# Step 0's first two pairs of an attention and feed-forward kernel: 64-key diagonal blocks and a carried state in place of full 128-key scores

## The chip, the cores and the metric

One core of one Trainium2 chip. The metric is the time of one execution on the device in microseconds; for the kernel before it is the median of 3 runs. The kernel is one program: every engine gets a fixed list of instructions, and semaphores make one engine wait for another.

## The reference

The first stage is a gated linear attention, B = 4, H = 8 heads, S = 768 positions, head size D = 48; the second a feed-forward layer on its output, 3072 tokens, 384 to 2048 to 384.

```
f = sigmoid(f_logit)
for t in range(S):
    state = f[t] * state + k[t] (outer) v[t]      # per batch and head, 48 x 48
    y[t] = q[t] @ state
x = y as (B * S, H * D)
h = x @ w_in
g = h where h >= 1, 0 where h <= -1, (h + 1)**2 / 4 between
out = g @ w_out
```

All inputs and the output are float32; the weights reach the chip as 64-bit words.

## The kernel before

**Steps, pairs, units.** Time is cut in 6 steps of 128 positions (C = 128, half of it T = 64). Heads go in 4 pairs per step, so pair n is pair n % 4 of step n // 4. A step's output is the x of the second stage, which is 16 units per step, one for every 128 columns of the hidden layer, so 96 units, numbered through. A unit is nine f16 products of 128x512 into `ph` (line 370, or 1041 for unit 0) and, two units later, nine into `po` (line 389). Attention of step i + 1 is put between the units of step i.

**How a pair is computed.** Gates make running products by scans on VectorE (lines 601 and 608), and keys and queries are multiplied by them (611, 613). For steps 1 to 5 two pairs go together: `both` (774) are the scores of 64 keys with 64 queries, in four diagonal blocks per batch; `parts` (978) sums keys times values over each half of the step; `begin` and `part` (863) are the masked scores times values of the second and of the first half; `before` (895) is the queries times the state that came before them. Between halves the state is handed on as `later`.

**Step 0 before the change.** It has no state before it, and its pairs 0 and 1 use full scores of 128 keys by 128 queries: `scores` (695), a mask on VectorE for each pair and head (739), and `first` (heads, 1007), the masked scores times values. Their keys are turned by TensorE (`turn`, 800) and kept, and `states(0)` makes the state for step 1 from them in one piece of 32 products (957), between units 4 and 5, with `states(2)`, for pairs 2 and 3, behind it. Pair 3 is spread over the rows of three gates: `last` (726) adds its scores up. `second` (1007 and 1019) is the values' part of pairs 2 and 3. The third gate (m = 2) is done in two halves of the batch, and so are the scores that need it.

**What sets the order.** A planner (class Plan) gives every operation a cost from the table COST, works out from the end how late each may be, and lets each engine take the ready one with the least slack. On TensorE every operation depends on the one that was added before it, so its order is the order in which the list START, then the units, then the places between units, name their work. TURNS says beside which unit a pair's keys are turned, VISITS at which units two pairs' scores and sums, their begin and their end stand (a half is behind that unit's second products), AFTER what else follows a unit. Where the planner expects TensorE to idle it puts in products of zeros (459). INSTRUCTIONS counts loads and products of a kind, since code comes in blocks.

```
START = (("scores", 0), ("mask", 0, 0), ("mask", 0, 1), ("last", 0), ("turn", 0), ("scores", 1), ("mask", 1, 0), ...
         ("scores", 2, 0), ("last", 2, 0), ("scores", 2, 1), ("last", 2, 1), ("first", 0),
         ("mask", 2, 1), ("mask", 3, 1), ("first", 1), ("second", 0), ("second", 2), ("mask", 2, 0), ("mask", 3, 0), ("second", 3))
INSTRUCTIONS = dict(scores=32, scores_half=16, heads=32, thirds=32, thirds_of_two=64, both=128, begin=64, ... parts=128, ... turn=8)
AFTER = {4.5: (('states', 0), ('states', 2)), 2: (('turn', 2), ('turn', 3))}
```

**Weights and their tests.** A weight piece comes by DMA (issued by SP, line 411), ScalarE takes its top byte (`bits`, 497), VectorE joins the rest (499), ScalarE rounds the high half (503), VectorE subtracts for the low half (504). Units need both. Besides, the fast path holds only if the inputs lie within bounds: `small_piece` loads each of the 16 weight blocks again, and four reductions each (523) find their least and greatest; `norms_of` squares on ScalarE, turns (822) and sums (823) on VectorE; the result is a flag that is read at the end. These are put wherever an engine is free.

Of the kernel before, what the change touches and what calls it, by code (L numbers as in the profile page):

```python
# [24 lines left out]
C = 128  # L25
NI = S // C
NP = H // 2
R = 112
# [31 lines left out]
W = 2 * DM  # L60


SMALL_PRODUCTS = ("scores", "scores_half", "heads", "thirds", "thirds_of_two", "both", "begin", "before", "before_half", "part", "states", "parts", "parts_last")
# [3 lines left out]
COST = dict(mm=216, narrow=114, scores=1000, scores_half=500, heads=940, thirds=940, thirds_of_two=940, half=330, both=940, begin=430, before=880, part=450, states=700, before_half=440, parts=730, parts_last=730, zeros=4860, turn=395, first=160, last=200,  # L67
            rows=316, turned_rows=150, scan=1140, dve=602, small=200, sums=467, gate=600, act=575, bits=660, round=485, copy=520, turned=412, sig=538, decay=226,
            issue=480, near=600, least=300)

# [10 lines left out]
def JOINED(n):  # L81
    return 65 + 1.055 * n


INSTRUCTIONS = dict(scores=32, scores_half=16, heads=32, thirds=32, thirds_of_two=64, both=128, begin=64, before=128, before_half=64, part=64, states=64, parts=128, parts_last=64, zeros=24, turn=8)
BLOCK, FIRST_BLOCK, AHEAD, BEHIND, FETCH, OFFSET, WAITS = 256, 193, 48, 40, 4800, 9, 1.0045


# [6 lines left out]
VISITS = {4: (7.0, 7.0, 11.0, 11.0), 6: (11.0, 12.5, 12.5, 12.5), 8: (22.0, 22.0, 24.5, 24.5), 10: (24.5, 27.5, 27.5, 27.5), 12: (33.0, 33.0, 37.0, 37.0), 14: (37.0, 43.5, 43.5, 43.5), 16: (48.0, 48.0, 51.0, 51.0), 18: (51.0, 55.5, 55.5, 55.5), 20: (68.0, 68.0, 75.0, 75.0), 22: (75.0, 75.0, 76.0, 76.0)}  # L95
# [29 lines left out]
class Plan:  # L125
# [7 lines left out]
    def add(self, engine, cost, emit, *deps, kb=0, count=None, many=0):  # L133
        flat, made = [], count is not None

        def spread(d):
            if isinstance(d, list):
                for e in d:
                    spread(e)
            elif d is not None and d not in flat:  # L140
                flat.append(d)

        spread(list(deps))
        cost, kind = COST[cost] if isinstance(cost, str) else cost, cost
# [12 lines left out]
        if engine == "PE":  # L157
            self.tensor = o
        self.ops.append(o)
        return o  # L160
# [96 lines left out]
def gla_moe(ctx: ExitStack, tc: tile.TileContext, ff, kqd, f0, vv, vad, vbd, wd, fixedd, gates, values, headsd, out):  # L257
# [75 lines left out]
    def wide(a):  # L333
        return a.rearrange("r b c -> r (b c)")
# [93 lines left out]
    def fresh(t):  # L428
        nc.gpsimd.memset(t, 0.0)
# [133 lines left out]
    def old(n, *names, of=att):  # L563

        return [] if n < 0 else [of[n].get(k) for k in names]
# [141 lines left out]
    am_of = [am[0:2], am[2:4], [am[0], act_f[0][:, 0:N].rearrange("r (b c) -> r b c", b=B)], [am[2], opening[2]]]  # L707
    last_held = [bank(6), bank(4)]

    def scores_of_last(t, some=ALL):  # L710
# [21 lines left out]
    def masks(n, h):  # L732

        c = att[n]
        c.setdefault("am", [None, None])
        b, ps, _ = c["held"][h]
        t = am_of[n][h]
        free = {(2, 0): lambda: att[0]["ys"][0], (3, 0): lambda: att[0]["ys"][0], }.get((n, h), lambda: None)
        o = vec("dve", lambda: nc.vector.tensor_tensor(
            out=t, in0=ps, in1=mask.rearrange("u (o t) -> u o t", o=1).broadcast_to([C, B, C]), op=ALU.mult),  # L740
            c["sc"], ready["mask"], free())
        banks[b][:] = [o]
        c["am"][h] = o

# [6 lines left out]
        return [by_block(t) for t in am[n // 2 % 2 * 2:][:2]]  # L751

    TILES = ((0, 0), (1, 1), (1, 0), (0, 1))

    def borrowed(k):

# [208 lines left out]
    def states_by_parts(n, k, alone):  # L965

        i, p = pairs[n]
        c, d = att[n], att[n + 1]
        held = [bank(0), bank(1)] if alone else borrowed(k)
        sums = [wide(b[1])[:R, 0:2 * B * D] for b in held]  # L970

        def emit():
            for e in range(2):
                for m, (q, t) in enumerate(blocks(n + e)):
                    a = (e * B + m) * D
                    for l, h in (TILES if i < NI - 1 else TILES[1:3]):
# [5 lines left out]
        o = vec("sums", lambda: nc.vector.tensor_tensor(out=later[:, 0:2 * B * D], in0=sums[0], in1=ds[n // 2 % 2][:, 0:2 * B * D], op=ALU.add),  # L982
                c["st"], c["db"], d["db"], old(n - 2, "y", "se"))
# [168 lines left out]
    for n in range(NP):  # L1152
        prepare(n)

    def of_first(t):
        att[0].setdefault("ys", []).append(heads(t, lambda m, e: va[:, m, 2 * e + t], [am_of[e][t] for e in range(2)], [att[e]["am"][t] for e in range(2)], [att[0]["lv"], banks[firsts[t][0]]]))
        att[0]["y"] = att[1]["y"] = att[0]["ys"][-1]
# [15 lines left out]
    work = dict(mask=masks, scores=lambda n, *h: scores(n, ((0, 1), (3, 2), (5, 7))[n], *[HALF[k] for k in h]), last=lambda t, *h: scores_of_last(t, *[HALF[k] for k in h]), first=of_first, second=of_second,  # L1173
                turn=lambda n: transpose_tensor(n, (5, 5, None, None)[n]), states=lambda n: states(n), rows=lambda n: transpose_rows(n))
    for kind, *n in START:
        work[kind](*n)
# [55 lines left out]
    for u in range(NI * NJ):  # L1232
        unit_1(u)
        attend(u)
        if u >= BEHIND_BY:
            unit_2(u - BEHIND_BY)
        attend(u + 0.5)
    for c in range(NJ):
        small_piece(c)
    for j in range(NJ):  # L1240
        norms_of(j)
    tested, again = test()
    fits = nc.alloc_registers("fits")
    registers = {r.engine: r for r in fits.handles}
# [166 lines left out]
```

## Time and profile before

| | |
|---|---|
| time, median of 3 runs | 444.78 us (444.38 to 445.21) |
| the profiled execution's own time | 444.19 us |
| its span, first to last instruction | 442.5 us |
| TensorE busy | 436.3 us, 99%, 4537 products and 4537 loads of weights |
| VectorE busy | 333.2 us, 75% |
| ScalarE busy | 223.8 us, 51% |
| GpSimd busy | 35.3 us, 8% |
| DMA | 53.30 MB, mean 120 GB/s |

The profile is of one execution. Products are pipelined: in a list in order of time, the step from one start to the next is what a product costs, and its printed length holds a run-out that the next one hides. A share of busy time says little of TensorE here; whether it waits is seen in the starts. Line numbers are those of the kernel before.

### The profile page before, as it was taken

The page shows a single profiled execution, that of the slowest core. Times are in us where ns is not written, and L with a number is a line of the kernel's source. Part 1 is how long each engine was busy: PE and PEld are TensorE (multiplying, and loading weights), DVE is VectorE, ACT ScalarE, POOL GpSimd, SP SyncE. Part 2 cuts the span into 40 slices and gives each one's busy share as a digit, 9 for nine tenths or more (in the row PEclk, how much of TensorE's full clock was granted, in tenths as well). Part 3 has the DMA queues.
Part 4 walks back from the last instruction along what each step waited for, and adds up shares of the span by engine and source line. Part 5 has one row for each costly group of instructions (what it writes and reads, how often), then busy time and mean ns, then how long its engine had stood idle before and what let it go on. Part 6 is the DMA issues. An engine that isn't in the chain of part 4 may idle for free.

```text
span 442.5 us, 10884 instructions
## 1 busy us (share of the span) xinstructions
PE 436.3 (99%) x4537; PEld 222.2 (50%) x4537; DVE 333.2 (75%) x664; ACT 223.8 (51%) x428; POOL 35.3 (8%) x77
## 2 busy tenths in 40 slices
PE   8999999999999999999999999999999999999996
PEld 4845545544554545544545545444444654444442
DVE  7979999899989898899999898499667836111111
ACT  4589899645535545355535274345434433533332
POOL 5103120102001011011001011000000000000000
PEclk9999999999999999999999999999999999999999
DMA  7879988542304413086322342171100000100002
GB/s 275 304 286 419 362 302 287 187 120 82 99 8 150 115 37 108 1 291 219 101 54 77 122 140 77 51 228 70 71 2 1 3 21 0 73 0 0 1 0 75
DMA packets 18003, 53.30 MB, mean 120 GB/s; under 512 B 3072, under 2 KB 3712, under 8 KB 17952
## 3 DMA queue, kind: packets, MB, share of 16 engines
q1 hardware_dynamic: 17952, 52.59, 34.9%
q8 instruction: 36, 0.59, 0.5%
q14 instruction: 15, 0.12, 0.1%
HBM read 44.70 MB, written 4.72 MB: 112 GB/s over the span
## 4 chain that ended last, share of the span: by engine, by line
PE 95%; DVE 0%; ACT 0%; issue 0%
PE po L389 42%; PE ph L370 42%; PE pa L863 2%; PE pa L895 2%; PE ph L774 2%; PE pa L978 1%; PE pa L800 1%; PE pa L774 0%; PE ph L1041 0%; PE pa L1007 0%; PE pa L957 0%; PE ph L978 0%; PE pa L1019 0%; PE po L1019 0%; DVE w_lo_usual L399 0%; ACT w_lo_usual L393 0%
## 5 line engine op out<-in xcount | busy, mean ns | idle before, releaser
L389 PE MATMUL po<-g_usual,w_hi_usual 128*128 128x512 f16 x866 | 201.9, 379 | 0.0
L382 ACT ACTIVATE act<-ph,lifted 128x512 f32<-128x512 f32 x96 | 65.8, 686 | 172.3 <-PE ph L370 169.6
L389 PEld LDWEIGHTS <-w_hi_usual 128*128 128x128 f16 x866 | 83.9, 98 | 100.0
L370 PEld LDWEIGHTS <-w_hi_usual 128*128 128x128 f16 x855 | 83.2, 98 | 99.4
L370 PE MATMUL ph<-x_usual,w_hi_usual 128*128 128x512 f16 x567 | 132.5, 379 | 0.0
L1058 DVE TENSOR_TENSOR g_usual<-act,g_usual 128x512 f16<-128x512 f32 x96 | 66.1, 689 | 79.2 <-ACT g_usual L1057 77.7
L814 DVE STREAM_TRANSPOSE kn<-kq 32x128 f32<-32x128 f32 x224 | 67.8, 302 | 3.3
L370 PE MATMUL ph<-w_lo_usual,w_hi_usual 128*128 128x512 f16 x288 | 67.4, 379 | 0.0
L1057 ACT CAST g_usual<-act 128x512 f16<-128x512 f32 x96 | 59.2, 617 | 2.4
L605 POOL COPY end<-w 128x4 f32<-128x4 f32 (+1 forms) x20 | 8.5, 426 | 227.3 <-DVE w L601 227.2
L601 DVE TENSOR_TENSOR_SCAN w<-f,least_w 128x512 f32<-128x512 f32 (+1 forms) x18 | 20.8, 1157 | 1.8 <-ACT f L597 1.8
L608 DVE TENSOR_TENSOR_SCAN f<-f,rec 128x512 f32<-128x512 f32 (+1 forms) x18 | 20.7, 1157 | 0.2
L523 DVE TENSOR_REDUCE ok<-raw 128x1 f32<-128x384 f32 x40 | 19.6, 536 | 0.0
L504 DVE SCALAR_TENSOR_TENSOR w_hi_usual<-bits,w_hi_usual 128x768 f16<-128x768 f32 (+1 forms) x20 | 15.6, 790 | 1.4 <-ACT w_hi_usual L503 1.4
L503 ACT ACTIVATE w_hi_usual<-bits 128x768 f16<-128x768 f32 (+1 forms) x20 | 14.0, 714 | 1.6 <-DVE bits L499 1.5
L618 POOL TENSOR_TENSOR kq<-end,f0s 128x4 f32<-128x4 f32 x18 | 13.4, 745 | 4.0 <-ACT f0s L581 2.5
L863 PE MATMUL pa<-am,v 64*64 64x64 f32 x624 | 13.6, 221 | 0.0
L863 PEld LDWEIGHTS pa<-am,v 64*64 64x64 f32 x624 | 11.3, 134 | 4.2 <-issue 3.8
L597 ACT ACTIVATE f<-f 128x513 f32<-128x513 f32 (+2 forms) x18 | 10.8, 603 | 4.7 <-DMA f<-in_f 4.7
L822 DVE STREAM_TRANSPOSE w_lo_usual<-w_lo_usual 128x384 f32<-128x384 f32 x22 | 12.6, 573 | 0.5
L393 ACT ACTIVATE w_lo_usual<-po 128x512 f32<-128x512 f32 (+1 forms) x18 | 10.5, 584 | 4.2 <-PE po L389 3.2
L611 DVE TENSOR_TENSOR kq<-kq,w 128x512 f32<-128x512 f32 (+1 forms) x20 | 12.4, 619 | 0.0
(137 smaller groups left out, 368.6 us busy)
## 6 DMA issues: line engine op xcount, KB each, us to landing
kq<-in_kq SPq DMA_DIRECT2D x18, 512.0 KB, 4.6
raw<-in_w SPq DMA_DIRECT2D x8, 767.6 KB, 7.0
raw<-in_w SPq DMA_DIRECT2D x7, 768.0 KB, 5.9
raw_late<-in_w SPq DMA_DIRECT2D x6, 768.0 KB, 4.3
out_y<-w_lo_usual SPq DMA_DIRECT2D x17, 256.0 KB, 2.1
f<-in_f SPq DMA_DIRECT2D x16, 256.5 KB, 3.2
v<-in_v SPq DMA_DIRECT2D x10, 384.0 KB, 4.5
raw_late<-in_w SPq DMA_DIRECT2D x4, 767.6 KB, 9.3
```

The lines of the kernel that those rows point to most:

```text
L370: nc.tensor.matmul(ps[:, to], w_in((ws or (w_hi, w_lo))[1 - high], j, kt), xt[t][:, kt, c], start=(n == 0), stop=(n == 8))
L382: nc.scalar.activation(a, ps, AF.Square, bias=lifted, scale=0.5 * 2.0 ** (UP_G // 2 - UP))
L389: nc.tensor.matmul(po[e][:, c], w_out((ws or (w_hi, w_lo))[part], j, e), g[:, c], start=(j == 0 and n == 0 and c.start == 0), stop=(j == N ...
L503: h = sca(ROUNDED(n), lambda: nc.scalar.activation(hi, val, AF.Copy, scale=2.0 ** UP_W), v)
L504: l = vec(JOINED(n), lambda: nc.vector.scalar_tensor_tensor(out=lo, in0=val, scalar=2.0 ** UP_W, in1=hi, op0=ALU.mult, op1=ALU.subtract), h)
L523: seen.append(vec(JOINED(DM), lambda at=at, op=op, b=b, e=e: nc.vector.tensor_reduce(out=ok[:, at:at + 1], in_=words_of(mem)[1][:, b:e].bi ...
L601: s1 = vec(COST["scan"] if count == 1 else 602, lambda bwd=bwd, u0=u0, u1=u1: nc.vector.tensor_tensor_scan(out=wide(w[:, u0:u1]), data0=bw ...
L608: s2 = vec(COST["scan"] if count == 1 else 602, lambda fwd=fwd, b0=b0, b1=b1: nc.vector.tensor_tensor_scan(out=fwd, data0=fwd, data1=wide( ...
L814: nc.vector.transpose(kn_of(n)[u:u + 32, ::-1, r:r + 32], src[:, :, u:u + 32])
L863: nc.tensor.matmul(held[h][1][64 * e:64 * e + 64, m, T * (1 - k):][:, :T], v_of[pr // 2][half, a:a + 64], masked(n)[h][half, block], start ...
L1057: o = g["hi"] = sca("copy", lambda: nc.scalar.copy(hi, a), o, unit_out.get(k - HOMES_G))
L1058: g["lo"] = vec("dve", lambda: nc.vector.tensor_tensor(out=lo, in0=a, in1=hi, op=ALU.subtract), o, unit_out.get(k - HOMES_G))
```

## The change

Pairs 0 and 1 of step 0 take the form of the later steps. Their scores are made in 64-key diagonal blocks for both pairs into the same two banks (`both_of_first`), with two masks for both pairs. `parts_of_first` sums keys times values over the two halves right in the opening; ScalarE copies the first half's sums twice (once padded, as the state that the second half's queries read) and the second half's once, and VectorE adds the two for step 1's state, so `states(0)` goes. `of_first` has three pieces: `begin`, `before` and `part`. The first warm-up is 10 products and two that clear the two banks. Loads and squares of the weights' tests wait until unit 64's first products are done. TURNS and VISITS get new numbers, for nearly all pairs.

```diff
-TURNS = {4: 6.5, 6: 10.5, 8: 21.0, 10: 26.5, 12: 32.5, 14: 41.5, 16: 46.0, 18: 51.5, 20: 60.5, 22: 72.5}
-VISITS = {4: (7.0, 7.0, 11.0, 11.0), 6: (11.0, 12.5, 12.5, 12.5), 8: (22.0, 22.0, 24.5, 24.5), 10: (24.5, 27.5, 27.5, 27.5), ...
-START = (("scores", 0), ("mask", 0, 0), ("mask", 0, 1), ("last", 0), ("turn", 0), ("scores", 1), ("mask", 1, 0), ("mask", 1, 1), ("turn", 1), ("last", 1),
-         ("scores", 2, 0), ("last", 2, 0), ("scores", 2, 1), ("last", 2, 1), ("first", 0),
-         ("mask", 2, 1), ("mask", 3, 1), ("first", 1), ("second", 0), ("second", 2), ("mask", 2, 0), ("mask", 3, 0), ("second", 3))
+TURNS = {4: 7.0, 6: 10.5, 8: 21.0, 10: 25.0, 12: 31.5, 14: 41.0, 16: 45.5, 18: 53.0, 20: 63.5, 22: 72.0}
+VISITS = {4: (8.0, 8.0, 11.0, 11.0), 6: (11.0, 12.5, 12.5, 12.5), 8: (22.0, 22.0, 23.5, 23.5), 10: (23.5, 26.5, 26.5, 26.5), ...
+START = (("last", 0), ("both", 0), ("turn", 0), ("turn", 1), ("both", 1), ("parts",), ("last", 1),
+         ("scores", 2, 0), ("last", 2, 0), ("first", "begin"), ("scores", 2, 1), ("last", 2, 1), ("first", "before"), ("first", "part"),
+         ("mask", 2, 1), ("mask", 3, 1), ("second", 0), ("mask", 2, 0), ("second", 2), ("mask", 3, 0), ("second", 3))
-AFTER = {4.5: (('states', 0), ('states', 2)), 2: (('turn', 2), ('turn', 3))}
+CHECKED = 4, 0
+WARM = 10
+AFTER = {4.5: (('states', 2),), 2: (('turn', 2), ('turn', 3))}
...
-    add("PE", "zeros", lambda: warm(12), set_zeros)
+    def cleared():
+        warm(WARM)
+        for t in (po[0], wide(pa[2])):
+            nc.tensor.matmul(t, zeros, zeros..., start=True, stop=True)
...
+    set_ds.append(add("POOL", 600, lambda: fresh(first_half)))
...
+    first_two = [bank(0), bank(1)]
+    def both_of_first(e):
+        def emit():
+            for m, (q, b) in enumerate(blocks(e)):
+                for k, h in TILES:
+                    (a, z), half = HEADS[h], slice(T * k, T * k + T)
+                    nc.tensor.matmul(by_block(first_two[h][1])[half, e * B + m], key(e, q, b)[a:z, half],
+                                     query(e, q, b)[a:z, T * (1 - k):][:, :T], start=True, stop=True)
+        c = att[e]
+        c["sc"] = add("PE", "both_half", emit, c["kq"])
+        if e == 0:
+            return
+        for h, (b, ps, _) in enumerate(first_two):
+            o = vec("dve", ... masked(0)[h] = by_block(ps) * mask_t ..., c["sc"], ready["mask_t"])
...
+    def parts_of_first():
+        held = [bank(3), bank(2)]
+        sums = [wide(b[1])[:R, 0:2 * B * D] for b in held]
...
+        c["st"] = d["st"] = add("PE", "parts", emit, c["kn"], d["kn"], c["lv"])
+        c["later"] = [sca(412, ... first_half[r:z, ...] = sums[0][r:z] ...) for (r, z), y in zip(HEADS, (0, PAD))]
+        c["sum"] = sca(412, lambda: nc.scalar.copy(later[:, 0:2 * B * D], sums[0]), c["st"])
+        c["rest"] = sca(412, lambda: nc.scalar.copy(second_half, sums[1]), c["st"])
+        banks[3], banks[2] = [c["later"], c["sum"]], [c["rest"]]
+    def of_first(what):
...
+        if what == "begin":
+            o = add("PE", "begin", lambda: attended_of(True), c["am"], c["lv"], banks[3], banks[2])
+            c["yb"] = sca("small", lambda: nc.scalar.copy(seen_y..., held[0][0:1, :, T - 2:T]), o)
+        elif what == "before":
+            c["ys"] = d["ys"] = add("PE", "before_half", before, c["yb"], c["later"], set_ds)
+        else:
+            c["y"] = d["y"] = add("PE", "part", lambda: attended_of(False), c["yb"])
+            o = vec("sums", ... state = second_half + later ..., c["y"], c["sum"], c["rest"])
...
+    first_of = len(plan.ops)
     for c in range(NJ):
         small_piece(c)
     for j in range(NJ):
         norms_of(j)
+    behind = unit_in[CHECKED]
+    for o in plan.ops[first_of:]:
+        if o.engine == "SP" or o.engine == "ACT":
+            o.deps.append(behind)
```

## Rows read from the trace of the kernel before

**Rows 1.** Busy time by stage: stretch, length, each engine's busy us, clock, DMA, GB/s
```profile
10.00:20.00 10.00, 9.17 (x138) 7.23 (x138) 10.00 (x22) 5.21 (x9) 2.57 (x6) 1.00 0.94 371
...
21.90:37.90 16.00, 16.00 (x79) 7.70 (x80) 13.47 (x23) 14.76 (x28) 0.99 (x1) 1.00 0.85 323
...
80.00:300.00 220.00, 220.00 (x2469) 110.57 (x2462) 196.17 (x426) 105.73 (x219) 18.96 (x36) 1.00 0.36 112
...
372.00:438.20 66.20, 66.20 (x309) 30.05 (x307) 12.29 (x19) 23.68 (x37) 0.00 (x0) 1.00 0.03 12
```

**Rows 2.** TensorE in order of time, 38 to 70 us: start, length, line, operation
```profile
38.23 0.93 PE L957 MATMUL pa<-sd,kn 128*48 128x48 f32 x32
38.99 0.89 PE L957 MATMUL pa<-v,am 128*48 128x48 f32 x32
...
47.59 0.93 PE L800 MATMUL pa<-ident,kq 112*128 112x112 f32 x8
48.36 2.11 PE L370 MATMUL ph<-x_usual,w_hi_usual 128*128 128x512 f16 x9
...
51.38 0.90 PE L978 MATMUL pa<-v,kn 64*48 64x48 f32 x64
52.21 2.12 PE L389 MATMUL po<-g_usual,w_hi_usual 128*128 128x512 f16 x9
...
68.63 0.69 PE L863 MATMUL pa<-am,v 64*64 64x64 f32 x32
69.14 0.22 PE L774 MATMUL ph<-kq 48*64 48x64 f32 x1
```

**Rows 3.** TensorE in order of time, 15 to 22 us, the opening's end
```profile
15.33 0.37 PE L695 MATMUL po<-kq 48*128 48x128 f32 x1
...
15.88 0.27 PE L726 MATMUL ph<-kq,w_lo_usual 64*128 64x128 f32 x1
...
16.53 1.09 PE L1007 MATMUL po<-am,sd 128*64 128x128 f32 x16
...
18.75 0.30 PE L1019 MATMUL po<-act,v 128*32 128x128 f32 x1
...
21.82 2.12 PE L1041 MATMUL ph<-x_usual,w_hi_usual 128*128 128x512 f16 x9
```

**Rows 4.** VectorE in order of time, 15 to 19 us: the first and the sixth mask
```profile
15.20 0.68 DVE L739 TENSOR_TENSOR am<-pa,fixed 128x512 f32<-128x512 f32 x1
...
18.19 0.68 DVE L739 TENSOR_TENSOR w_lo_usual<-po,fixed 128x512 f32<-128x512 f32 x1
```

**Rows 5.** Line 895 from 69.5 to 73 us: least, median, greatest ns, first and last start
```profile
L895 PE MATMUL pa<-kq,later x32: 218/218/218, 70.1 to 70.5; 48*64 48x64 f32 x32
```

**Rows 6.** ScalarE in order of time near 40 us: the copy behind states(0)
```profile
40.28 0.47 ACT L961 COPY sd<-pa 112x384 f32<-112x384 f32 x1
```

**Rows 7.** TensorE in order of time: first products of units 64 and 80
```profile
302.03 2.11 PE L370 MATMUL ph<-x_usual,w_hi_usual 128*128 128x512 f16 x9
...
372.04 2.10 PE L370 MATMUL ph<-x_usual,w_hi_usual 128*128 128x512 f16 x9
```

**Rows 8.** The tests: line 523 behind 300 us by stage; groups of 822 and 823
```profile
300.00:443.00 143.00, 9.63 (x20) 1.00 0.06 22
...
L822 DVE STREAM_TRANSPOSE w_lo_usual<-w_lo_usual 128x384 f32<-128x384 f32 x22 | 12.6, 573 | 0.5
...
L823 DVE TENSOR_REDUCE w_lo_usual<-w_lo_usual 128x4 f32<-128x384 f32 x22 | 12.0, 547 | 0.4
```

**Rows 9.** ScalarE and VectorE in order of time, 43 to 49 us: unit 7's weights
```profile
43.39 1.00 ACT L497 ACTIVATE bits<-raw_late,top_of 128x768 uint32<-128x768 fp8e4 x1
...
46.19 0.93 DVE L499 SCALAR_TENSOR_TENSOR bits<-raw_late,bits 128x768 uint32<-128x768 uint32 x1
...
47.34 0.86 ACT L503 ACTIVATE w_hi_usual<-bits 128x768 f16<-128x768 f32 x1
```

**Rows 10.** The page's DMA queues: packets, MB, share; TensorE's code
```profile
q8 instruction: 36, 0.59, 0.5%
```

More of the change, by code (lines that the diff above doesn't have):

```diff
@@ L60 @@
 W = 2 * DM
-SMALL_PRODUCTS = ("scores", "scores_half", "heads", "thirds", "thirds_of_two", "both", "begin", "before", "before_half", "part", "states", "parts", "parts_last")
+SMALL_PRODUCTS = ("scores", "scores_half", "heads", "thirds", "thirds_of_two", "both", "both_half", "begin", "before", "before_half", "part", "states", "parts", "parts_last")
 HOP, LANDING, PER_KB, LANES, FIRST, RISE = 200, 1350, 2.75, 8, 500, 700
 LATENCY = dict(PE=235, ACT=140, DVE=110, POOL=150)
-COST = dict(mm=216, narrow=114, scores=1000, scores_half=500, heads=940, thirds=940, thirds_of_two=940, half=330, both=940, begin=430, before=880, part=450, states=700, before_half=440, parts=730, parts_last=730, zeros=4860, turn=395, first=160, last=200,
+COST = dict(mm=216, narrow=114, scores=1000, scores_half=500, heads=940, thirds=940, thirds_of_two=940, half=330, both=940, both_half=470, begin=430, before=880, part=450, states=700, before_half=440, parts=730, parts_last=730, zeros=4860, turn=395, first=160, last=200,
             rows=316, turned_rows=150, scan=1140, dve=602, small=200, sums=467, gate=600, act=575, bits=660, round=485, copy=520, turned=412, sig=538, decay=226,
@@ L82, in JOINED @@
     return 65 + 1.055 * n
-INSTRUCTIONS = dict(scores=32, scores_half=16, heads=32, thirds=32, thirds_of_two=64, both=128, begin=64, before=128, before_half=64, part=64, states=64, parts=128, parts_last=64, zeros=24, turn=8)
+INSTRUCTIONS = dict(scores=32, scores_half=16, heads=32, thirds=32, thirds_of_two=64, both=128, both_half=64, begin=64, before=128, before_half=64, part=64, states=64, parts=128, parts_last=64, zeros=24, turn=8)
 BLOCK, FIRST_BLOCK, AHEAD, BEHIND, FETCH, OFFSET, WAITS = 256, 193, 48, 40, 4800, 9, 1.0045
@@ L737, in masks @@
         t = am_of[n][h]
-        free = {(2, 0): lambda: att[0]["ys"][0], (3, 0): lambda: att[0]["ys"][0], }.get((n, h), lambda: None)
         o = vec("dve", lambda: nc.vector.tensor_tensor(
             out=t, in0=ps, in1=mask.rearrange("u (o t) -> u o t", o=1).broadcast_to([C, B, C]), op=ALU.mult),
-            c["sc"], ready["mask"], free())
+            c["sc"], ready["mask"])
         banks[b][:] = [o]
@@ new lines, in parts_of_first, with emit @@
+    def parts_of_first():
+        c, d = att[0], att[1]
+        held = [bank(3), bank(2)]
+        sums = [wide(b[1])[:R, 0:2 * B * D] for b in held]
+        def emit():
+            for e in range(2):
+                for m in range(B):
+                    a = (e * B + m) * D
+                    for l, h in TILES:
+                        (r, z), half = HEADS[h], slice(T * l, T * l + T)
+                        nc.tensor.matmul(sums[1 - l][r:z, a:a + D], kn_of(e)[half, m, r:z], values_of(e, h)(m)[half], start=True, stop=True)
+        c["st"] = d["st"] = add("PE", "parts", emit, c["kn"], d["kn"], c["lv"])
+        c["later"] = [sca(412, lambda r=r, z=z, y=y: nc.scalar.copy(first_half[r:z, :, y:y + D], sums[0][r:z].rearrange("r (g c) -> r g c", c=D)), c["st"], set_ds)
+                      for (r, z), y in zip(HEADS, (0, PAD))]
+        c["sum"] = sca(412, lambda: nc.scalar.copy(later[:, 0:2 * B * D], sums[0]), c["st"])
+        c["rest"] = sca(412, lambda: nc.scalar.copy(second_half, sums[1]), c["st"])
+        banks[3], banks[2] = [c["later"], c["sum"]], [c["rest"]]
@@ new lines, in of_first, with attended_of, before @@
+    def of_first(what):
+        c, d = att[0], att[1]
+        held = [f[1] for f in firsts[:2]]
+        def attended_of(other):
+            for m in range(B):
+                for e, k in TILES:
+                    h, half = 1 - k if other else k, slice(T * k, T * k + T)
+                    nc.tensor.matmul(held[h][64 * e:64 * e + 64, m, T * (1 - k):][:, :T], va[half, m, 2 * e + h], masked(0)[h][half, e * B + m],
+                                     start=other and m == 0, stop=m == B - 1, skip_group_check=not other)
+        def before():
+            for m in range(B):
+                for e, h in TILES:
+                    (r, z), (q, b) = HEADS[h], blocks(e)[m]
+                    nc.tensor.matmul(held[h][64 * e:64 * e + 64, m, T:], first_half[r:z, e * B + m], query(e, q, b)[r:z, T:], start=False, stop=False, skip_group_check=True)
+        if what == "begin":
+            o = add("PE", "begin", lambda: attended_of(True), c["am"], c["lv"], banks[3], banks[2])
+            c["yb"] = sca("small", lambda: nc.scalar.copy(seen_y.rearrange("u (b c) -> u b c", b=B), held[0][0:1, :, T - 2:T]), o)
+            c["yb"].early = PROMPT
+        elif what == "before":
+            c["ys"] = d["ys"] = add("PE", "before_half", before, c["yb"], c["later"], set_ds)
+        else:
+            c["y"] = d["y"] = add("PE", "part", lambda: attended_of(False), c["yb"])
+            s = state[:, 0:2 * B].rearrange("r b e -> r (b e)")
+            o = vec("sums", lambda: nc.vector.tensor_tensor(out=s, in0=second_half, in1=later[:, 0:2 * B * D], op=ALU.add), c["y"], c["sum"], c["rest"])
+            c["se"] = d["se"] = state_of[0, 0] = [o]
@@ L1171, in of_second @@
             x_of[0, t] = rounded(firsts[t][0], wide(firsts[t][1]), lambda t=t: [x_at(0)[n][:, t] for n in range(2)], y, None)
-    work = dict(mask=masks, scores=lambda n, *h: scores(n, ((0, 1), (3, 2), (5, 7))[n], *[HALF[k] for k in h]), last=lambda t, *h: scores_of_last(t, *[HALF[k] for k in h]), first=of_first, second=of_second,
+    work = dict(mask=masks, both=both_of_first, parts=parts_of_first, scores=lambda n, *h: scores(n, ((0, 1), (3, 2), (5, 7))[n], *[HALF[k] for k in h]), last=lambda t, *h: scores_of_last(t, *[HALF[k] for k in h]), first=of_first, second=of_second,
                 turn=lambda n: transpose_tensor(n, (5, 5, None, None)[n]), states=lambda n: states(n), rows=lambda n: transpose_rows(n))
```

20 lines of the change are left out of this document (14 added, 6 removed).

## The prediction

> **What bounds the kernel now.** First the table of stages: behind 21.9 us TensorE is busy for every microsecond of a stretch (16.00 of 16, 220.00 of 220, 66.20 of 66.2), at the full granted clock, 2.4 GHz [rows 1]. The reader then goes to the order of products, because a busy share hides stalls: the nine products of the unit at 48.36 take 2.11 us with the last one's run-out, and no gap stands between a unit and the small products beside it [rows 2]. So behind the first product of unit 0, at 21.82 [rows 3], the time is a plain sum of what TensorE issues, plus an end (438.2 to the last instruction) that the change leaves alone. Two things alone can move the time: what is taken out of that sum or held up within it, and the moment at which unit 0 begins.
>
> What sets that moment is read from VectorE: it is busy for 10.00 of the 10 us from 10 to 20 [rows 1]. At 15.20, right behind the third gate's last product, it begins to mask scores; the masks are 0.60 apart, (18.19 - 15.20) / 5 [rows 4]. TensorE waits for them: `first` for head 0 starts at 16.53, just behind the second mask, and `second` at 18.75, just behind the sixth; then it runs through to unit 0 in 21.82 - 18.75 = 3.07 us [rows 3]. There are eight masks in all.
>
> **The change, part by part.**
>
> *The states of pairs 0 and 1 leave the stream.* `states(0)` ran between units 4 and 5, from 38.23 to 38.99; `states(2)` follows it directly and stays [rows 2]. With the stream gapless, 0.76 us go. The switch into and out of small products is paid by `states(2)` as before. The new places move small products between units, but their number and kind stay: each pair of pairs still has its visit, its begin and its end, and the turns of pairs 4 to 7 stay on TensorE. I cost that at nothing as long as their inputs come in time (rivals).
>
> *The opening on TensorE.* Removed: two full scores and two `first` groups. Added: two `both_half`, one `parts`, `begin`, `before_half`, `part`. Their prices stand in the stream: `parts` 52.21 - 51.38 = 0.83, `begin` or `part` 69.14 - 68.63 = 0.51 [rows 2], `before_half` 0.45 from its 32 starts between 70.1 and 70.5 [rows 5]. What lies early is hidden: pair 1's keys, not TensorE, decide when the second `both_half` can start, and `parts` follows in a stretch in which TensorE before did whole scores. What lies behind the third gate counts.
>
> *The opening on VectorE.* Pairs 0 and 1 need two masks where they needed four: 1.20 us less. But TensorE's order is a chain, and `begin`, which reads those two masks, stands in it ahead of the second half of the third gate's scores. So both masks come before the last scan and products of gate 2, and push them: the second half of scores can start not at 15.33 but at about 15.33 + 2 x 0.60 = 16.53. From there TensorE issues half scores 0.55 (15.33 to 15.88 [rows 3]), half of the last pair's 0.44 to 0.65 (below: as many products of the same width at the pitch of the half before it, less its start; above: 15.88 to 16.53 with its wait; I take 0.55), `before_half` 0.45, `part` 0.51: 2.06 us, and `second` starts at 18.59 instead of 18.75. VectorE agrees: those scores are out some 0.8 us after they start, two masks follow, 16.53 + 0.8 + 1.20 = 18.53. So of the 1.20 us that VectorE saves, 0.6 to 0.8 are lost waiting for scores that now come later, and TensorE's chain takes most of the rest. Behind 18.75 nothing changes (3.07 us). Unit 0 begins about 0.15 us earlier; between 0 (the wait of 0.65 and one more switch of product form) and 1.20 (all of VectorE's saving arrives).
>
> *ScalarE.* Four copies out of PSUM (two of the first half's sums, its second copy, the other half) replace the one of `states(0)`, which takes 0.47 at 40.28 [rows 6]; the copies for `begin` must also have emptied the two banks into which it writes. Four times 0.47 is 1.9 us behind `parts`, which can end near 13.5 (estimate: pair 1's keys near 11.4, `both_half`, a turned copy, 0.83). `begin` could then start near 15.4, about when its masks are done, and end near 15.9; it has until 16.53. Cost 0; without that cover up to 0.6.
>
> *Sum on VectorE, clears.* The added `sums` runs behind `part`, is read by step 1 only, and takes the place of ScalarE's copy: 0. The two clearing products replace two warm ones: 0. The memset of `first_half` on GpSimd has some 10 us before its reader: 0.
>
> *The tests of the weights.* Loads and squares now wait for unit 64, which starts at 302.03 [rows 7]. Of 64 reductions 20 ran behind 300 already, 9.63 us; the 44 others, at the same price 21 us, move there, and with them squares' sums, at most (12.6 + 12.0) us [rows 8]. From 372 to 438.2 VectorE is busy for 12.29 of 66.2 us [rows 1]: there is room, and the result is wanted only at the end. On SP a test's load that waits for a free buffer holds up what is queued behind it, the gathers of step 5 among them; their unit starts at 372.04 [rows 7], long after they can be issued. What it frees, VectorE time between 68 and 300, is worth nothing by itself, since TensorE waits for nothing there (220.00 of 220 us from 80 to 300) [rows 1]. Cost 0, gain 0; below and above by the risk of a late step, up to 0.5 us either way.
>
> *Sum.* 0.76 + 0.15 = 0.91. The profiled execution took 444.19 us (span 442.5 and 1.7 around it), so 443.28; it lies 0.59 under the median of 444.78, and against that the forecast is 443.87, say 443.85.
>
> **Rivals.**
>
> A, *the whole of VectorE's saving arrives*: the masks of pairs 0 and 1 fit in where VectorE would wait anyway, the second half of gate 2 stays at 15.2, and `second` begins 0.6 to 1.20 earlier. For it: the scores for these masks are ready near 12.5. Against: VectorE has no idle time there [rows 1]. 444.78 - 0.76 - (0.6 to 1.20) = 442.8 to 443.4.
>
> B, *the weights of unit 7 come late* (slower). Their high half is written by ScalarE at 47.34 + 0.86 = 48.20 [rows 9], and unit 7's first product is at 48.36 [rows 2]: 0.16 to spare. TensorE would now be there 0.15 + 0.76 earlier, and also without the turn of pairs 4 and 5 (48.36 - 47.59 = 0.77 [rows 2]), whose place moves from 6.5 to 7.0, behind unit 7. It asks for the weights 1.68 earlier; if they stay, it stands for 1.52 and the time is 444.78 - 0.91 + 1.52 = 445.4. It turns the sign once the stall passes 0.91. For it: VectorE is full in that stretch, and ScalarE nearly. Against: the raw bits were ready at 43.39 + 1.00 and VectorE joined them only at 46.19 [rows 9], 1.8 us of choice, spent on gates of pair 4 whose visit moves a unit later too. If unit 8 is also late it is worse, to 446.
>
> C, *TensorE's instructions arrive late in the opening*. By the kernel's own table the list START issues 720 loads and products where it issued 400. Code comes as packets: 36 of them, 0.59 MB [rows 10], about one for 252 of TensorE's instructions. The blocks that it needs are now reached some 4 us earlier, while DMA is full. A stall in `begin` is hidden for 0.6 us; past that it would be 0 to 1.5 us, an estimate from the 4 us less the 2.5 us of other work between: 443.9 to 445.4, middle 444.6. Against: `parts` issues 128 in 0.83 us in the stream [rows 2] without a stall behind it.
> The Trainium skill ("Runtime: NRT & Kernel Launch", section Instruction fetch mechanics) says that the sequencer fetches the next 16 KiB block of 256 instructions while it executes the current one, and that this is hidden because dispatch is slower than the fills. By that rule C has no price and the time stays 443.85; the packet count and the gapless stream agree with it, but no row here shows it in an opening this dense, so C keeps its chance.
>
> **How the numbers follow.** A difference under 0.2% (0.89 us) can't be told from none by this kernel's measurement. My forecast 0.54, its own range 443.4 to 444.4, which the 0.2% line at 443.89 cuts near the middle: 0.30 faster, 0.24 same. A 0.16, all faster. B 0.17: 0.09 same, 0.08 slower (a stall near 1.8 is needed). C 0.13: 0.09 same, 0.04 slower. Together faster 0.46, same 0.42, slower 0.12. The range reaches from A's middle, widened to 442.9, to B's 445.3.
>
> **What would show it.** In the changed trace: one group of 32 products of `states` where there were two; the second half of pair 2's scores near 16.5 and two masks right before gate 2's last scan; `second` near 18.6 and unit 0 near 21.7; no gap over 0.1 us at units 4 to 9. A unit 0 before 21.2 makes A right. A gap before unit 7 or 8 makes B right, one inside `begin` or `before_half`, with a code packet that ends with it, C. The forecast is wrong if unit 0 begins after 21.9, or if TensorE's stream from unit 0 to its end is not 0.7 to 0.8 us shorter.

## The result and the profile after

The changed kernel takes 448.2 us (median of 6 runs, 446.91 to 449.23), the one before 445.03 (6 runs, 444.38 to 445.21): ratio 1.0077, interval 1.0063 to 1.0092. It is slower; the forecast was 443.85. The profiled execution took 449.16 us, its span is 447.4, 4.9 more than before. Line numbers are each kernel's own; `begin` and `part` are L816 here, `before_half` L823, half scores L702, `second` L1101, unit 0 L1123.

Stream first. TensorE of the changed kernel in order of time (start, length, engine, line, operation, count), the first products of units 64 and 80, then the group of the one `states` that is left (least, median, greatest ns, first and last start):

```profile
306.95 0.81 PE L372 MATMUL ph<-x_usual,w_hi_usual 128*128 128x512 f16 x3
...
376.99 0.81 PE L372 MATMUL ph<-x_usual,w_hi_usual 128*128 128x512 f16 x3
```

```profile
L1039 PE MATMUL pa<-v,am x32: 207/208/243, 43.9 to 44.6; 128*48 128x48 f32 x32
```

Unit 64 was at 302.03 and unit 80 at 372.04 [rows 7]: 4.92 and 4.95 later. All of the loss is there before unit 64. The opening, same view:

```profile
15.45 0.37 PE L702 MATMUL po<-kq 48*128 48x128 f32 x1 [0.28 <-DVE kq L620]
...
16.54 0.27 PE L816 MATMUL pa<-am,sd 64*64 64x64 f32 x1
...
16.77 0.22 PE L816 MATMUL po<-am,sd 64*64 64x64 f32 x1
18.94 0.37 PE L816 MATMUL pa<-am,sd 64*64 64x64 f32 x1 [1.95 <-issue]
...
19.77 0.58 PE L702 MATMUL po<-kq 48*128 48x128 f32 x1
...
21.78 0.36 PE L823 MATMUL po<-kq,w_lo_usual 48*64 48x64 f32 x1
...
27.49 0.82 PE L1123 MATMUL ph<-x_usual,w_hi_usual 128*128 128x512 f16 x3
```

Unit 0 starts at 27.49 where it was at 21.82 [rows 3]: 5.67 later, of which the stream gives back 5.67 - 4.92 = 0.75. In the middle of the 32 products of `begin` TensorE stands from 16.77 to 18.94, and "issue" says that the profile shows no engine and no data for which it waited. What it waited for is seen in the queue of TensorE's code, here as the DMA queues (packets, MB, share) list it from 16.3 to 16.5 us. From 13.0 to 16.2 that queue has no packet; the one below starts at 16.36, takes 1.02, and ends 1.56 us before the next product:

```profile
q8 instruction: 1, 0.02, 31.8%
```

and in the table of stages (stretch, length, busy us of PE, PEld, DVE, ACT, POOL, clock, DMA share, GB/s):

```profile
12.00:16.00 4.00, 3.71 (x127) 3.23 (x126) 4.00 (x11) 3.21 (x8) 1.52 (x4) 1.00 1.01 411
16.00:18.00 2.00, 0.99 (x24) 0.73 (x20) 1.89 (x5) 1.13 (x3) 0.00 (x0) 1.00 1.02 389
18.00:20.00 2.00, 1.06 (x22) 0.95 (x24) 0.00 (x0) 0.11 (x2) 0.00 (x0) 0.71 1.04 342
20.00:22.00 2.00, 2.00 (x24) 1.78 (x28) 0.79 (x2) 2.00 (x5) 0.00 (x0) 0.50 0.62 208
...
24.00:26.00 2.00, 2.00 (x40) 1.53 (x34) 1.19 (x3) 0.32 (x1) 0.00 (x0) 0.59 0.28 33
26.00:28.00 2.00, 2.00 (x33) 1.59 (x29) 1.69 (x3) 1.98 (x5) 0.00 (x0) 1.00 0.77 219
```

Two things to see. DMA is full (1.01 to 1.04) up to 20 us. And at the end of the standstill the granted clock goes to 0.50, which is 1.2 GHz, and is back at 1.00 only shortly before 26 us: the rest of `begin`, half scores, `before_half`, `part` and most of `second` run at half speed. VectorE in order of time dates the third gate, and its waits (waited for: us in total, times, longest) show one that before did not have up to 18 us:

```profile
15.31 0.68 DVE L780 TENSOR_TENSOR am<-pa,fixed 128x512 f32<-128x512 f32 x1
...
17.03 0.42 DVE L620 TENSOR_TENSOR kq<-kq,act 128x256 f32<-128x256 f32 x1
17.37 0.55 DVE L506 SCALAR_TENSOR_TENSOR bits<-raw_late,bits 128x384 uint32<-128x384 uint32 x1
```

```profile
DVE kq L618 <- DMA kq<-in_kq: 0.7, 1, 0.7
```

The 5.67 add up. The gate ends at 17.37 instead of 15.20 [rows 4]: +2.17, which is the two masks put ahead, 1.20 as forecast, and 0.97 of lateness, 0.7 of it that wait. The second half of the scores could follow 0.13 later (15.33 - 15.20 before) at 17.50 and starts at 19.77: +2.27 by the standstill, some 0.33 of it half clock in what was left of `begin` (0.83 from 18.94 on, 0.50 with the clock full in two experiments below). From there to unit 0 it takes 7.72 us, where before took 6.49. At full clock and without gaps it takes 5.22 (two experiments below), so the shorter chain gives -1.27 and the half clock takes +2.50. 2.17 + 2.27 - 1.27 + 2.50 = 5.67. This is the sum of one execution: where the clock stayed full, `second` stood 1.48 us instead (below).

### The profile page after: what moved, and what is told of

Read it like the earlier page. It is cut to its first block, busy times and chain, and to the rows that moved or that the text cites. A ratio compares the mean times of both kernels' runs of the same rounds, so it can differ in the third digit from the quotient of the medians.

```text
span 447.4 us, 11149 instructions
## 1 busy us (share of the span) xinstructions
PE 438.5 (98%) x4667; PEld 223.7 (50%) x4667; DVE 331.6 (74%) x663; ACT 224.3 (50%) x432; POOL 31.7 (7%) x78
## 4 chain that ended last, share of the span: by engine, by line
PE 95%; DVE 2%; DMA 1%; issue 1%; SPq 0%; ACT 0%; DVEq 0%
PE po L391 42%; PE ph L372 41%; PE pa L945 2%; PE pa L977 2%; PE ph L856 2%; PE pa L1060 1%; DMA f<-in_f 1%; DVE w L608 1%; PE pa L882 1%; PE pa L856 0%; PE ph L1123 0%; PE po L702 0%; PE po L1101 0%; PE ph L1060 0%; PE pa L816 0%
## 5 line engine op out<-in xcount | busy, mean ns | idle before, releaser
L618 DVE TENSOR_TENSOR kq<-kq,w 128x512 f32<-128x512 f32 (+1 forms) x20 | 12.3, 620 | 2.9 <-DMA kq<-in_kq 2.9
L868 DVE TENSOR_TENSOR am<-ph,fixed 128x512 f32<-128x512 f32 x10 | 6.9, 690 | 9.8 <-PE pa L856 9.8
```

## The experiments

The theory, **late code**: TensorE's instructions come in packets (about one for 252 of them [rows 10]; the planner counts 256), and the instructions of one packet are a block. Each block is asked for while TensorE runs the one before; with DMA full of weights, values and gates the packet starts late, and the opening, 720 instructions now where it had 400, comes to the end of its block, a border, and stands. Rivals: the standstill is the switch between product forms in `begin`, or a wait for data or a bank that the profile doesn't name; the loss comes from the tests or the places; the code comes late however DMA stands, since the opening is too dense. In the expectations F is late code, T the tests, and D the rival that the expectation names.

**The tests late, alone** (on the kernel before) and **the new places with them**:

```
+    behind = unit_in[4, 0]
+    for o in plan.ops[first_of:]:           # loads and squares of the tests
+        if o.engine == "SP" or o.engine == "ACT": o.deps.append(behind) ...
```
```
+TURNS, VISITS = those of the changed kernel
```

> The kernel before with one part of the change alone: loads and squares of the weights' tests wait for unit 64. Theory F (TensorE's code block for the opening's dense small products arrives late, and begin stands still for it) and theory D (begin waits for data or a bank that the trace doesn't name) both expect no difference from before, 444.8 to 445.3. Theory T (the late tests cost the time) expects 447 to 448.5.

> The kernel before with the late tests and with the change's TURNS and VISITS, but with the opening and states(0) of before. F: as before, 444.4 to 445.2, unit 0 at 21.8, no gap in the stream. The rival of late weights (unit 7 asks for its weights 0.77 us earlier, as the turn of pairs 4 and 5 moves behind it): a gap of up to 0.6 us ahead of unit 7, time 445 to 446.

444.47 against 444.61, ratio 0.9998 (0.9988 to 1.0007); and 444.30 against 444.34, ratio 1.0000 (0.9991 to 1.0009). Neither edit costs or gains anything that can be measured. With both, the waits of TensorE in the whole span are one, for the zeros of the warm-up, so unit 7's weights are not late:

```profile
PE ph L459 <- DVE zeros L424: 1.2, 1, 1.2
```

**The change with the tests early:**

```
-        if o.engine == "SP" or o.engine == "ACT":
+        if False:
```

> The changed kernel with the weights' tests placed as before the change (no wait for unit 64); the opening is the changed one. Theory F (code for the opening comes late): as the changed kernel, 446.9 to 449.2, with the gap of 1.5 to 2.3 us in begin. Theory T: 445 to 445.5. Its profile also shows the opening a second time: if TensorE's clock stays at full speed behind the gap, unit 0 is near 25 and the span near 445; if it falls to half, near 27 and 447.

449.13 against 444.34, ratio 1.0107 (1.0077 to 1.0138). The loss stays. Waits of TensorE:

```profile
PE pa L816 <- issue: 1.4, 1, 1.4
PE pa L1101 <- issue: 1.2, 1, 1.2
...
PE pa L977 <- issue: 0.9, 1, 0.9
```

In this profile the clock stayed full and two blocks are seen to be late: 1.59 us in `begin` (from start to start), 1.48 in `second`. From the second half's scores to unit 0 it took 25.01 - 18.31 = 6.70, less 1.48 of gap 5.22. The third wait, in `before` at 81.77, the changed kernel does not have; DMA was full there, with test loads that come late in the changed kernel.

**Code asked for earlier.** 72 tiny products of zeros behind the warm-up let the block borders fall 144 instructions earlier; in the other kernel 56 more behind unit 5 make it 256, so that the borders of the stream stand where they were.

```
+        for _ in range(EARLY):                     # 72, in the warm-up
+            nc.tensor.matmul(ph[1][0:1, 0:1], zeros[:, 0:1], zeros[:, 0:1], start=True, stop=True)
...
+        if u == PAD_AT: add("PE", 30 * LATER, padding, held, count=2 * LATER)   # unit 5, 56 more
```

> As the one with 72 early tiny products, but without the 56 later ones: every later block boundary of TensorE's code falls 144 instructions earlier against the groups of small products. F: the gap in begin is gone, but several gaps of 0.5 to 3 us appear inside dense groups between units, time 450 to 470. D: no new gaps in the stream, time as the changed kernel, 447.5 to 449.5.

> The changed kernel with 72 tiny products of zeros (one row, one column; 144 instructions) in the first warm-up and 56 more behind unit 5's first products, so that block boundaries of TensorE's code lie 144 instructions earlier in the opening and at their old places (256 on) from unit 5 on. F: no gap inside begin; the next boundary now falls into before_half, where up to 1 us may be lost; unit 0 near 22 to 23.5; the 56 later products cost some 1.5 us; time 444.5 to 446.5. D: the gap of 2.2 us in begin stays, unit 0 near 27, time 449 to 450.

With both, 448.23 against 444.61, ratio 1.0087 (1.0066 to 1.0107): `begin` ran through from 16.75 to 17.23 and the standstill moved on to `before_half`, 1.47 us. A switch of product form does not move with the count, nor does a wait for data or a bank; a block border does. The time stayed long all the same: unit 0 was at 24.04 (2.22 later than before), the 56 products took some 1.5, and one unit waited 1.0 for its weights; less the 0.75 of the stream that is some 4.0 of the 4.2 us by which this span is longer.

```profile
PE pa L828 <- issue: 1.2, 1, 1.2
```

The 72 alone cost most of all: 460.74, ratio 1.0382 (1.0351 to 1.0413). With the borders shifted, nine standstills of 1.1 to 1.8 us stand in the dense groups or right behind them, all along the stream. Its waits:

```profile
PE pa L980 <- issue: 5.3, 4, 1.5
PE pa L948 <- issue: 3.3, 3, 1.1
PE pa L826 <- issue: 1.8, 1, 1.8
```

So where the borders fall is worth many microseconds to this kernel, and the planner that chose the places reckons with them.

**DMA emptied.** Two kernels asked only for a later place of some loads in SP's order, and failed at that: the weights were still issued near 8 us and DMA stayed full, 1.00 to 1.05 from 8 to 16 us.

```
-        loaded = dma(into, ..., last_in.get(home))
+        loaded = dma(into, ..., last_in.get(home), att[0]["yb"] if 2 <= k < 5 else None)   # the second kernel: k < 5
...                                       # the same for gates 3 and 4; in the second kernel for the values too
```

> The changed kernel with five loads held back until begin is done: weight pieces 2 to 4 and the gates of step 1's first two pairs (some 1.7 MB that before filled DMA from 8 to 18 us). No instruction of TensorE is added or moved. F: with DMA less full the code packet comes sooner, the gap in begin falls from 2.2 us to under 1, time 445 to 446.5. D: gap and time stay, 447.5 to 449.

> The changed kernel with every load that nothing in the opening up to begin reads held back until begin is done: weight pieces 0 to 4, the values of pairs 2 and 3, the gates of step 1's first pairs (some 3 MB). second and unit 0 then wait for their own data, so the time itself says little (449 to 453); what counts is begin. F with full DMA as the reason: the code packet starts within 2 us of both_half, the gap in begin falls under 0.7 us. If a block takes its 5 us whatever DMA does: the gap stays at 1.5 us or more.

The first took 447.77, ratio 1.0079 (1.0062 to 1.0096): `begin` stood 1.55 us, `second` 1.48, the clock stayed full, unit 0 at 24.56; 24.56 - 17.86 - 1.48 = 5.22 again. The second (447.72, one run) stood 2.00 us in `begin`, and 1.6 us behind it the clock fell to 0.50 once more. Both together with the early code:

```
+EARLY, LATER = 78, 44        # and the loads of the first of the two
```

> The changed kernel with 78 tiny products early and 44 behind unit 5, and five loads held back until begin is done (both of the earlier edits, and the planner told of the early ones). It shows what the opening is worth with little waiting for code. F: no gap in begin, at most 1 us in before_half, scores (2, 1) near 16.6 to 17.2, unit 0 at 21.7 to 23, time 444.6 to 446.5 with 1.2 us for the 44 products and up to 0.8 for weights that come later. D: the gap in begin is back, unit 0 near 25, time over 447.5.

451.39, ratio 1.0153 (1.0134 to 1.0172). `begin` ran through, `before_half` stood 0.87, unit 0 was at 23.22; 122 products are not a whole block, and standstills of 1.3 (listed as a wait for ScalarE), 1.5 and 1.7 us in the stream took more than the opening won.

Then the loads were held by data: a copy on GpSimd behind `begin` writes one element into each buffer, so the load has to come after it.

```
+    def touched(t): return add("POOL", 200, lambda: nc.gpsimd.tensor_copy(out=t, in_=seen_y[0:1, 0:1]), att[0]["yb"])
+    held_back = {k: touched(raw[(k + 3) % 5]...) for k in range(5)}    # the other kernel: (2, 3, 4)
+    held_gates = {m: touched(f[(m - 1) % 2][0:1, 0:1]) for m in (3, 4)}
+    o = touched(vb[0:1, 0, 0:1])                                       # the values; not in the other kernel
```

> The changed kernel; a GpSimd copy behind begin writes one element into the buffers of weight pieces 0 to 4, of the values of pairs 2 and 3 and of step 1's first gates, so that their loads (some 3 MB) really wait for begin: in the run before, which only asked for a later place, SP reached the loads without a wait and DMA stayed full to 18 us. second and unit 0 will wait for their data (time 452 to 456). Theory F with full DMA as the reason: DMA falls under half from some 12 us, the code packet starts within 2 us of the second both_half (about 12), begin has no gap over 0.5 us. If a block takes its time whatever DMA does: the packet again starts near 15 and the gap is 1.5 to 2.2 us.

> The changed kernel with weight pieces 2 to 4 and step 1's first gates held by data until begin is done (1.7 MB). If DMA is then free before the packet is asked for, begin runs through and the time is 444 to 446; if DMA is full until 14 us all the same, the gap shrinks to about 1 us and, as weights come later, the time is 446 to 448.

The first of the two decides on the opening. With everything held, stages, the code's queue from 12.3 to 12.6 us, and TensorE in order of time:

```profile
10.00:11.00 1.00, 1.00 (x9) 0.67 (x8) 1.00 (x3) 0.42 (x1) 0.67 (x2) 1.00 0.49 176
11.00:12.00 1.00, 1.00 (x22) 0.70 (x24) 0.96 (x3) 0.90 (x3) 0.04 (x1) 1.00 0.00 0
12.00:13.00 1.00, 1.00 (x94) 1.00 (x84) 1.00 (x4) 0.86 (x2) 0.14 (x1) 1.00 0.07 16
```

```profile
q8 instruction: 1, 0.02, 23.3%
```

```profile
12.24 0.20 PE L799 MATMUL pa<-sd,kn 64*48 64x48 f32 x1
...
15.13 0.27 PE L817 MATMUL pa<-am,sd 64*64 64x64 f32 x1
...
15.60 0.22 PE L817 MATMUL po<-am,sd 64*64 64x64 f32 x1
16.77 0.37 PE L703 MATMUL po<-kq 48*128 48x128 f32 x1 [0.95 <-DVE kq L621]
...
18.38 0.22 PE L817 MATMUL po<-am,sd 64*64 64x64 f32 x1
25.66 0.39 PE L1102 MATMUL po<-act,v 128*32 128x128 f32 x1 [6.63 <-DMA v<-in_vb]
```

The packet comes just behind the start of `parts` (12.24), where in the changed kernel `parts` starts at 13.17 and the packet at 16.3 or later. The same products, as dense as before, run through `begin` in 0.47 us without a standstill: in this opening it is full DMA that makes the code late. (The 452.70 us of this run are those of the held values, awaited until 25.66; they say nothing on the change.) With only some loads held DMA was full until 14 us, and the time 447.24, ratio 1.0067 (1.0051 to 1.0084), as the second branch expected: `begin` stood 1.07, `second` 1.48:

```profile
PE pa L1102 <- issue: 1.2, 1, 1.2
...
PE pa L817 <- issue: 0.9, 1, 0.9
```

**The disputed cost by itself.** On the kernel before, 256 products of one column, 512 instructions, behind unit 58, where DMA is nearly idle, and behind unit 6, where it is full. They are added work; the rest is untouched.

```
+        if u == BURST_AT:          # 58; in the other kernel 6
...
+            add("PE", 26 * BURST, burst, held, count=2 * BURST)     # BURST = 256
```

> The kernel before with 256 tiny products of zeros (512 loads and products, exactly two blocks of code) behind unit 58's first products, in a stretch without other small products. F: the burst runs at some 26 ns a product until it comes to a block that was asked for only inside the burst; there it stands for 2 to 3 us, once or twice; burst and gaps 8.5 to 12 us, time 453.5 to 457. D (dense small products issue at their own pace): 256 x 0.026 = 6.7 us without a gap, time 451.5.

> The same burst of 256 tiny products (512 instructions) in the kernel before, now behind unit 6's first products, near 45 us, where DMA is full (1.02); near 281 us, with DMA mostly idle, it ran through in 6.4 us. F with full DMA: one or two gaps of 1 to 2.5 us each in the burst, which takes 8 to 11 us. If DMA has no part in it: 6.4 us again.

453.93 and 455.20 us, one run each (before beside them 444.34 and 444.50). Behind unit 58, by stage and in order of time:

```profile
281.10:284.30 3.20, 3.20 (x129) 3.20 (x129) 1.65 (x5) 1.31 (x2) 0.00 (x0) 1.00 0.02 6
284.30:287.50 3.20, 3.20 (x134) 3.20 (x130) 3.19 (x7) 0.00 (x0) 0.00 (x0) 0.84 0.13 22
287.50:290.00 2.50, 2.50 (x12) 0.93 (x9) 2.50 (x7) 0.00 (x0) 0.00 (x0) 0.50 0.72 190
```

```profile
281.10 6.54 PE L1235 MATMUL pa<-zeros 128*1 128x1 bf16 x256
287.58 4.02 PE L390 MATMUL po<-g_usual,w_hi_usual 128*128 128x512 f16 x9
```

and behind unit 6:

```profile
45.00:48.00 3.00, 3.00 (x86) 2.28 (x84) 3.00 (x6) 2.74 (x5) 1.47 (x3) 1.00 1.00 411
48.00:51.00 3.00, 3.00 (x127) 3.00 (x124) 3.00 (x5) 3.00 (x9) 0.96 (x1) 1.00 1.02 400
51.00:54.00 3.00, 0.68 (x28) 0.58 (x25) 3.00 (x5) 2.37 (x7) 0.00 (x0) 0.57 1.01 316
```

```profile
46.02 5.36 PE L1235 MATMUL pa<-zeros 128*1 128x1 bf16 x209
...
53.70 1.31 PE L1235 MATMUL pa<-zeros 128*1 128x1 bf16 x47 [2.32 <-issue]
```

The same two blocks at the same density pass in 6.5 us without a gap where the DMA share is 0.02 to 0.13, and stand 2.5 us (51.22 to 53.70) where it is 1.0. At this density, 25 ns a product (129 in 3.20 us), full DMA is what it takes.

It is not what it takes everywhere. `parts` and the groups beside it are nearly twice as dense, 13 to 15 ns a product (`parts` takes 0.83 us for 64), and the kernel with the 72 early products alone stands in such groups where DMA is idle. By stage and in order of time:

```profile
217.00:219.00 2.00, 2.00 (x158) 2.00 (x161) 0.67 (x2) 1.32 (x3) 0.00 (x0) 1.00 0.04 8
219.00:221.00 2.00, 0.46 (x31) 0.36 (x26) 1.96 (x6) 0.00 (x0) 0.00 (x0) 1.00 0.00 0
```

```profile
219.05 0.30 PE L980 MATMUL pa<-kq,later 48*64 48x64 f32 x8
220.88 0.58 PE L980 MATMUL pa<-kq,later 48*64 48x64 f32 x24 [1.54 <-issue]
```

The one packet between 217 and 219 us is code, and it starts at 218.25, 0.9 us before TensorE stands. At all nine of its standstills the DMA share of the 2 us before is at most 0.10. From the start of the packet to the next product these nine take 2.4 to 2.7 us. By these figures (an estimate) the 128 products of a block last 1.7 us at 13 ns and 3.2 us at 25 ns, so groups as dense as these run out too soon even with DMA idle, while the burst does so only where full DMA makes the packet start late.

**A smaller version.** The gain in the stream without the dense opening: `states(0)` of the kernel before, moved behind the last pair's scores, 64 instructions more in the opening; then with the tests late.

```
-         ..., ("last", 2, 1), ("first", 0),
+         ..., ("last", 2, 1), ("states", 0, 0), ("first", 0),
```

> A version that draws on F: the kernel before with states(0), 32 products and 64 instructions, moved from behind unit 4 into the opening, between last (2, 1) and first (0), where TensorE waits for masks. The next code block is then wanted only at the third of the second groups, some 7 us after it was asked for. F: no gap; second starts at 19.0 instead of 18.75, 0.76 us leave the stream; time 444.0 to 444.5 against 444.6 to 445. If 64 more instructions in the opening already cost a wait for code: a gap near 20 to 21 us and 445 to 446.5.

> The kernel before with states(0) in the opening, as the earlier version, and with the change's late tests. In the earlier version the gap of 1.34 us at 79.4 lay at a code block whose packet began at 78.5 while DMA was full (1.03), with a load of the tests under way from 70.7. Theory F (code comes late where the 256 instructions of a block run out before the packet for the next, which waits behind full DMA): without the tests' loads that gap goes; unit 0 starts at 22.1 to 22.3, 0.76 us leave the stream, time 0.3 to 0.6 us under before. If DMA has no part in it, the gap stays and the time is 445 to 446.

445.85 against 444.34, ratio 1.0034 (1.0019 to 1.0049), and 444.71 against 444.24, ratio 1.0007 (0.9998 to 1.0016). The opening has no standstill, but unit 0 starts at 22.23 and 22.30, which takes back 0.41 and 0.48 of the 0.76. The first also stands in `before` at 79 us (L895, 1.1 us). From 76 to 78 us, first without and then with the tests late:

```profile
76.00:78.00 2.00, 2.00 (x36) 0.99 (x38) 1.96 (x3) 2.00 (x4) 0.00 (x0) 1.00 1.03 331
```

```profile
76.00:78.00 2.00, 2.00 (x40) 0.99 (x41) 1.75 (x4) 2.00 (x4) 0.00 (x0) 1.00 0.04 16
```

The loads of the tests keep DMA full there, and the code packet starts at 78.48; without them it starts at 75.75, and the standstill is gone. No version beat the kernel before: at unit 64 the profile of the second is level with it (302.01 against 302.03), so the rest of the 0.76 is not seen either.

## Why the prediction was wrong, by its own steps

**The stream** (-0.76): right, -0.75 and -0.72 at units 64 and 80.

**Tests late and new places** (0): right, 0 for the first alone and 0 for both. Rival B did not come: with the new places unit 7 asks for its weights 0.77 earlier and does not wait. The 1.68 earlier of the prediction was not reached in any run, as unit 0 came late in every changed kernel, so that much is untested. Not seen in the prediction: the late tests keep DMA free for code near 80 us, worth about 1 us once the borders are moved.

**The opening's arithmetic** (unit 0 at 21.67): its form was right. With code in time the second half's scores start at 16.77 (forecast 16.53) and `part` at 18.38 (16.53 + 0.55 + 0.55 + 0.45 = 18.08); from those scores to unit 0 it is 5.22 where the terms 2.06 + 3.07 gave 5.13. Rival A is refuted: the masks do push the gate. What the sum left out is the gate's lateness in the changed kernel, 0.97, of which 0.7 is a wait for keys by DMA. It is no fixed price: in the first kernel that asked for a later place of five loads the keys come without that wait, and the gate ends at 16.41, 1.21 behind 15.20 where the two masks gave 1.20. Why the keys landed later in the one and not in the other no run asked.

**Rival C** is the step that failed. The sum has no term for code, and the rival priced it too low: "stall in `begin` is hidden for 0.6 us; past that it would be 0 to 1.5 us", with a chance of 0.13. The mechanism and its place were right, and the sign "a code packet that ends with it" nearly so (the packet ends 1.56 us before the standstill does); the price and the chance were wrong, in three ways. It priced one block, and 720 instructions against 400 are more than one block further: in three kernels whose clock stayed full two are late, 1.1 to 1.6 us in `begin` and 1.48 in `second`; in the profiled execution the one in `begin` is 2.17. It took the time to fetch from the 4 us by which the blocks are reached earlier, without a row that shows a fetch; in the changed kernel the packet starts some 3 us behind the point at which it starts with DMA idle, and the product behind the standstill starts 18.94 - 13.3 = 5.6 us after that point (13.17 + 12.38 - 12.24 = 13.3). And nothing in it counted the clock. The argument against it, `parts` issuing 128 in 0.83 us without a stall, compared with a stretch whose borders lie elsewhere. The kernel itself held a price: its planner counts 4800 ns from asking for a block to its arrival (FETCH, line 86 of the kernel before). Taken from 13.3, a point that only the runs gave, that is 18.1 and a standstill of 1.3 us; the prediction read the counts beside it and not that number.
The Trainium skill ("Runtime: NRT & Kernel Launch", section Instruction fetch mechanics) says that fetching is hidden because dispatch is slower than the fills. The burst behind unit 58 agrees (no gap). The one behind unit 6 and the opening do not (2.5 and 2.2 us), nor do the dense groups of the kernel with the early code alone (1.1 to 1.8 us with DMA idle). The measurement decides: here the fetch is hidden only where a block takes longer than it does.

**What stays open.** How much of the 3.2 us is the half clock. The six runs of the changed kernel have spans of 445.2 to 447.5 us at mean granted clocks of 0.990 to 1.000, but the order of the two is not the same; the profiled execution had 2.50 us of it behind the scores, while three variants (the tests early, five loads asked for later, some loads held by data) had none in their profiles and took 447.24 to 449.13 us all the same. For the late block in `second` DMA's part is not shown: where DMA was emptied, `second` waited for its values. Nor is it known why some 1.2 to 1.6 us pass, with DMA full or idle, between the end of a packet (16.36 + 1.02 in the changed kernel) and the next product (18.94).

## What to carry to other kernels

Where an engine's instructions are dense, count them per block: a border passed there cost 1 to 2.5 us with DMA full and, in the densest groups, 1.1 to 1.8 us with DMA idle. A gap of that kind says "issue" in the waits, with a code packet that ends inside it or shortly before it. Work moved out of a smooth stream into an opening that shares DMA with the first loads can cost more than it frees. Edits that shift the number of instructions by anything but a whole block move every border behind them.

## What the runs showed of the hardware that was not expected

A code packet starts later when DMA is full: 16 KB that start 0.14 us behind the first product of `parts` with DMA at 0.00 to 0.07 start 2.1 to 3.1 us later than that in the five kernels with the same opening and a full DMA (0.94 to 1.05 from 12 to 14 us). And TensorE's clock fell while 256 one-column products kept it busy without a gap (0.84 in the burst's second half): the nine products behind them take 4.02 us, at a granted clock of 0.50, where a unit's nine take 2.11 [rows 2]. In the burst behind unit 6 it fell when the standstill had hardly begun (51.22; the granted clock is 1.00 from 51.2 to 51.4 us and 0.57 from 51.4 to 51.6), so there too it may be the burst's doing and not the standstill's. In the openings the clock fell at the end of a standstill of 2.2 us, 1.6 us behind one of 2.0, and within the wait of 6.63 for held values, but not behind one of 2.05 us at 18.85 with the early code alone, where it stays at 1.00: the length of a standstill by itself does not tell.
